# Two attention blocks, twice: the same operations issued in another order

## The chip, the core and the metric

The kernel runs on one core of one Trainium2 chip. The core has four engines that compute: TensorE (PE in the profile; PEld are its weight loads), VectorE (DVE), ScalarE (ACT) and GpSimd (POOL). SyncE (SP) issues most DMAs. Each engine works through its own instructions strictly in the order in which they were written, and waits at a semaphore where an instruction needs what another engine has yet to make. The metric is the device time of one execution in microseconds (us); lower is better. A time given for a kernel is the median of its runs.

## The reference

The input `x` has 2048 rows of 512 numbers, bf16. Four residual layers follow each other: A, B, A, B. Each normalises the rows, projects them to q, k and v for 32 heads of 16 columns, mixes, and projects back.

```python
x = x + A(layernorm(x))     # softmax attention over a window of 256 rows, causal
x = x + B(layernorm(x))     # linear attention: phi(q) @ sum(phi(k)^T v) / (phi(q) . sum(phi(k)))
x = x + A(layernorm(x))     # the same weights as the first A
x = x + B(layernorm(x))     # the same weights as the first B
# phi(t) = (t + 1 if t > 0 else exp(t)) + 1e-6
```

In layer A a row sees only 256 earlier rows, so the next B can begin on rows whose A is done. A row of B, though, needs the sum over all rows, so B's second half (dividing and projecting back) waits for the end of B's first half.

## The kernel before

The rows are cut into 16 tiles of 128, and four tiles make a block of 512; there are four blocks (I = 0 to 3) in each layer. Weights and the residual `xres` stay in SBUF. PSUM is one tensor `psb` of eight banks.

**A layer, block by block.** `ln_tile` (L661 and L662 statistics, L595 and L596 the inverse root on POOL) or `ln_sums` (L612 to L628) normalises a tile into `xn`; a DMA or PE transposes it into `xnT`. `proj` (L537) multiplies by a weight: four matmuls of 512 columns each into one bank, written as two half-steps of two matmuls that may stand apart. `evac` (L527) copies the bank out, on ACT or DVE; for the values it writes `vst`, for the queries `qT`. `k_spread` and `k_unit` (L773, L788) write the keys to `kall`; SP scatters the values from `vst` to `vbd` (L806).

**Scores and mixing.** A round of `scores` is one run of windows of 64 keys: PE multiplies keys and queries into four banks (L823), ACT takes the exponential of two banks (L834) and of the other two (L837), into one of seven buffers `pt`. Windows at the edge of the mask are set to zero: on POOL, one `affine_select` for each window (L857), or on DVE, one multiply by `tri` for one or two windows (L852). `pv_group` (L880) then multiplies `pt` by `vbd`, four steps of up to 12 small matmuls for a pair of tiles, and DVE divides (L893, L894) into `o_sb`, which is projected back and added to `xres` (L736 to L740). There are 156 rounds, 78 in each A layer. PE can begin a round when the exponentials of earlier rounds have emptied the four banks that it takes; ACT can begin the round's exponentials when PE is through with it.

**B layer.** Keys, values and queries are projected, `phi` is an exponential on ACT (L948), a clamp on DVE or POOL (L951) and a combination on DVE (L954). `kv_unit` (L995) sums keys times values; `kv_final` (L1042, L1051, L1063) makes the matrix `wkv` from it; `norm_pair` and `norm_unit` (L1078 to L1110) divide; `p2_tile` projects back, and in the last layer the rows go out (L720 to L731).

**What sets the order.** All of this is first noted down as 2583 operations with their needs, their possible engines and the buffers they take. Then `Planner.run` reads the string `ORDER` and issues them one by one. In it `692A` is operation 692 on ACT; the letters P, A, V, G and S stand for PE, ACT, DVE, POOL and SP; digits behind the letter are the buffers taken (for PE, mostly banks). `2F7` is no operation of the network: `fill` issues two matmuls of the identity into bank 7 (L463), whose result nobody reads. Nothing is reordered later, so the string alone fixes what stands behind what on each engine, which engine takes an operation that may go to several, and which bank or buffer it uses.

Four stages are spoken of below, cut at the start of a round on PE in the trace: the first A from its first round (10.9 us) to round 66 (135.1), the passage through B into the second A up to round 78 (135.1 to 205.7), the second A up to its last round (205.7 to 365.4), and the last B up to the end.

Of the kernel before, what the change touches and what calls it, by code (L numbers as in the profile page):

```python
# [214 lines left out]
24S 2G 5G 4G 15H 14H 53V0 0G 11G 58V1 17H 54A 68A1 6G 16H 63V2 3G 59G 55V20 18H 19H 1G 10F0 56P5 60V0 64G 61P1 57A 62V  # L215
9G 69V 2F2 74P0 75A 7V 1F2 70P1 65V0 72P6 71A 66P3 20H 92P7 73A 21H 67V 93P 120P42 94A 80P0 122A 95S 76P6 81V 88P1 121A
77V 89P 23H 22H 78P2 350V0 90A 123G 124P64 82P0 126A 79V 351G 91S 84P1 125A 340V1 133P24 83A 127G 96P6 85V 134A 106P0
10G 97V 104P1 135A 107V 137P26 341G 105V 139A 86P0 138A 146P46 87V 27S 116P1 147A 335V2 98P0 117P 148A 99V 336G 150P42
136V 25S 112P0 345V3 151A 149G 113P 152A 159P64 118A 337V31 140G 102P2 114V 161A 35S 128P1 346G 129P 103V 130P 131P 160A
342V1 163P42 153G 132V 26H 165A 115S 347V2 162G 3F0 188P06 164A 634V1 100P2 189A 166G 141P5 154P4 101V 155P 142P 36H  # L220
143P 190A 635G 144P 28H 352V0 193P02 145V 156P 119S 12G 157P 194A 108P6 158V 167P7 168P 191G 169P 195A 109V 170P 199P04
171V 348P6 200A 353P3 196G 349V 338P7 172S0 354V 343P6 201A 339V 204P02 638V0 379P7 29S 205A 380P 202G 344V 636V32 192G
206A 381V 2F5 210P04 361P6 639G 637S 642V1 362P 211A 208G 110P7 363V 212A 31S 203G 224P02 30H 198G 640V0 225A 383P5 213G
111V 384P 197V 382S 226A 643G 229P06 385V 214P4 215P 230A 646V0 216P 32H 358P5 644V3 231A 647G 217P 228V 235P02 641S
218V 359P 209G 236A 207G 355P7 360V 219P6 645S 237A 933V2 240P04 356P 241A 648V1 220P 239G 357V 221P 649S 232G 222P 233G
242A 246P02 227V 387P7 234G 386S 247A 223V 388P 238G 245V 389V 248A 395P04 13G 664P6 396A 665P 249V 934G 390S 250P7 667V
251P 397A 244G 400P02 666V 252P 243G 401A 941V0 253P 399G 391P6 392P 254V 402A 176S1 405P04 393V 364P7 406A 403G 365P
255P6 407A 366V 394S 410P02 256P 398V 257P 411A 404V 409G 258P 678P7 259V 412A 679P 416P04 680V 260S3 417A 657P3 414G
408V 415G 658P 276V 418A 650P2 264S2 660V 432P06 651P 413V 434A 419G 420V 51S 367P5 421V 368P 433A 659V 422P4 423P 369V
# [12 lines left out]
977P6 742A 554V 746P40 978P 748A 544P7 979V 545P 747A 744V 752P20 980S 745V 958P6 575V 754A 959P 750G 546V 735G 749V
269G 753A 2F5 768P40 960V 185G 751V 769A 755V 2F7 773P62 756V 757V 8V 774A 186G2 763P5 758P4 764P 567V0 775A 759P 187S
765P 559V1 760P 770A 766P 776G 761P 777G 275S 767V 778P26 270G1 955P0 779A 762V 956P 556P1 780A 957V 976S 783P42 557P
784A 782G 961P7 558V 962P 771G 785A 789P04 963V 985P6 271S 781G 790A 986P 786G 987V 791A 788G 183S 2F3 805P20 772G 787V
806A 793V 2F7 810P64 794G 37S 792V 812A 800P3 801P 802P 807A 795P5 803P 796P 811A 804V 797P 798P 571V2 38H 815P02 329P6
40H 813G 816A 46H 808G 799V 311P7 44H 50H 330P 560G 817A 52H 820P40 42H 331V 312P 821A 561G22 317P6 313V 822A 826P24
819V 809G 562S 318P 827A 548P7 824G 319V 549P 818G 823V 825G 828A 989P02 550V 814G 990A 831V 2F6 994P46 829G 830V 568G
995A 832P1 833P 834P 991A 835P 837P5 836V 838P 996A 839P 563V1 840P 842S0 1000P02 320A0 323P7 998G 841V 1001A 324P 564G
854S2 981P6 325V 1002A 1005P04 569G0 982P 999V 321V 1006A 964P7 983V 992G 965P 850S3 1007A 967P3 966V 1004G 968P 572G  # L250
332A3 1011P06 846S1 969V 843P5 1012A 1003G 844P 993G 855P4 1008V 984S 1013A 997G 1025P02 845V 856P 1010G 1009V 1027A
282P73 857V 283P 1026A 1014V 1030P24 858V3 277P62 570S 1031A 1015P0 322V 278P 988S 1016P 573V1 1032A 1017P 284V 1018P
279A 1036P24 1034G 1019V 1020P7 1038A 1021P 280V 1022P 281V 1023P 1037A 1041P04 1035V 290P60 1024V 1043A 291P 1040G
# [1195 lines left out]
```

## Time and profile before

| | before |
|---|---|
| time, median of 3 runs (lowest to highest) | 416.57 us (415.88 to 417.28) |
| profiled execution: span from first to last instruction | 414.3 us |
| median of the runs less that span | 2.3 us |
| busy PE / ACT / DVE / POOL | 395.2 / 368.8 / 355.0 / 239.2 us |
| mean granted clock of TensorE | 0.997 |

The profile is of one execution, whose own whole time is not listed; the 2.3 us beside its span is what lies around the first and last instruction if it was an ordinary one. Busy time of PE is the time in which some matmul is under way; as matmuls overlap, a PE that is busy may still be running with pauses. A stage's own figures say more than those of the whole: an engine that is busy for nearly all of a stage sets its length, whatever it does in others.

### The profile page before, as it was taken

How to read it: one execution, taken by the hardware profiler on the slowest of the kernel's cores; microseconds unless marked ns; L12 is line 12 of the kernel's file. 1: busy time of each engine (PE TensorE's matmuls, PEld its weight loads, DVE VectorE, ACT ScalarE, POOL GpSimd, SP SyncE). 2: the span in 40 equal slices, each digit the busy share in tenths (PEclk: the TensorE clock that was granted, in tenths of full speed). 3: DMA queues.
4: the chain of work that ended last, by engine and by line, in shares of the span. 5: the costliest groups of instructions: out<-in, count | busy, mean ns of one | idle time of the engine just before them, and what ended most of it. 6: DMA issues, size and time to landing. Idle time of an engine off the chain costs nothing.

```text
span 414.3 us, 15373 instructions
## 1 busy us (share of the span) xinstructions
PE 395.2 (95%) x6277; PEld 219.3 (53%) x6347; DVE 355.0 (86%) x844; ACT 368.8 (89%) x496; POOL 239.2 (58%) x505
## 2 busy tenths in 40 slices
PE   7998999999999999999999999999999999999995
PEld 3565555555555555643565555555555555565342
DVE  5899898888769988689998999998789588889895
ACT  5999999999999999678999999999999999977731
POOL 7578524344576667923774688554427476585432
PEclk9999999999999999999999999999999999999998
DMA  8233226440313122100032212322111311300024
GB/s 245 83 95 100 64 76 110 110 77 24 89 25 80 35 55 26 28 4 0 22 72 41 55 45 64 71 38 53 41 49 34 54 30 40 54 14 14 3 69 138
DMA packets 65306, 24.11 MB, mean 58 GB/s; under 512 B 46160, under 2 KB 65232, under 8 KB 65232
## 3 DMA queue, kind: packets, MB, share of 16 engines
q1 hardware_dynamic: 63168, 21.65, 23.5%
q10 hardware_dynamic: 2064, 1.44, 1.1%
q8 instruction: 50, 0.82, 0.8%
q14 instruction: 24, 0.20, 0.2%
HBM read 6.29 MB, written 2.10 MB: 20 GB/s over the span
## 4 chain that ended last, share of the span: by engine, by line
PE 66%; ACT 15%; DVE 12%; issue 4%; POOL 2%; ACTq 0%; POOLq 0%; DVEq 0%
PE psb L537 41%; PE psb L880 14%; PE psb L823 8%; ACT pt L834 7%; ACT pt L837 7%; DVE pt L852 2%; DVE kall L788 1%; PE psb L995 1%; DVE qT L527 1%; PE psb L566 1%; DVE kall L773 1%; PE psb L463 1%; DVE vst L527 1%; PE psb L1106 1%; DVE ln L661 1%
## 5 line engine op out<-in xcount | busy, mean ns | idle before, releaser
L857 POOL TENSOR_SCALAR_AFFINE_SELECT pt<-pt 128x256 bf16<-128x256 bf16 x285 | 121.3, 453 | 110.2 <-ACT pt L837 66.7
L837 ACT ACTIVATE pt<-psb 128x1024 bf16<-128x1024 f32 (+2 forms) x156 | 156.2, 1017 | 4.4 <-PE psb L823 3.0
L834 ACT ACTIVATE pt<-psb 128x1024 bf16<-128x1024 f32 (+2 forms) x156 | 156.7, 1014 | 3.6 <-PE psb L823 2.3
L880 PEld LDWEIGHTS <-pt 128*128 128x128 bf16 x2880 | 81.4, 96 | 16.5 <-issue 5.0
L880 PE MATMUL psb<-vbd,pt 128*128 128x34 bf16 x2880 | 85.1, 178 | 2.4 <-ACT pt L834 1.0
L537 PE MATMUL psb<-xnT,wA 128*128 128x512 bf16 (+1 forms) x305 | 65.1, 335 | 2.2 <-DVE o_sb L894 0.3
L537 PE MATMUL psb<-wB,xnT 128*128 128x512 bf16 x237 | 62.4, 379 | 1.7 <-issue 0.5
L823 PE MATMUL psb<-qT,kall 32*128 32x256 bf16 (+4 forms) x1664 | 62.6, 242 | 0.6 <-ACT pt L834 0.4
L537 PEld LDWEIGHTS <-xnT 128*128 128x128 bf16 x384 | 33.4, 97 | 37.0 <-issue 5.3
L823 PEld LDWEIGHTS <-kall 32*128 32x128 bf16 x1664 | 28.0, 92 | 45.8 <-issue 42.2
L852 DVE TENSOR_TENSOR pt<-pt,tri 128x512 bf16<-128x512 bf16 (+1 forms) x133 | 49.5, 399 | 2.8 <-ACT pt L837 1.9
L537 PEld LDWEIGHTS <-wA 128*128 128x128 bf16 x320 | 27.4, 97 | 26.1 <-issue 7.7
L537 PE MATMUL psb<-woA,oT 128*128 128x512 bf16 x120 | 32.8, 380 | 1.2 <-issue 0.6
L537 PE MATMUL psb<-wA,xnT 128*128 128x512 bf16 x115 | 32.3, 380 | 1.5 <-ACT pt L837 0.5
L537 PE MATMUL psb<-xnT,wB 128*128 128x512 bf16 x119 | 32.1, 380 | 0.9 <-issue 0.5
L537 PE MATMUL psb<-wkv,pqT 128*128 128x512 bf16 (+1 forms) x126 | 30.2, 373 | 0.5 <-issue 0.2
L894 DVE TENSOR_TENSOR o_sb<-psb,rall 128x256 bf16<-128x256 f32 x64 | 27.2, 424 | 2.4 <-DVE rall L893 0.2
L893 DVE RECIPROCAL rall<-psb 128x16 f32<-128x16 f32 x64 | 16.1, 251 | 13.7 <-PE psb L880 9.4
L661 DVE BATCH_NORM_STATS2 ln<-xres 128x6 f32<-128x512 f32 (+1 forms) x39 | 26.6, 682 | 1.2 <-DMA xres<-in_A_x_dram 1.1
L596 POOL TENSOR_TENSOR ln<-ln,mhalf 128x1 f32<-128x1 f32 x38 | 22.0, 578 | 3.2
L948 ACT ACTIVATE pks<-psb 128x512 bf16<-128x512 f32 x32 | 19.5, 614 | 3.8 <-PE psb L537 3.4
L527 DVE CAST qT<-psb 128x512 bf16<-128x512 f32 (+1 forms) x32 | 19.2, 602 | 3.9 <-PE psb L537 3.7
(133 smaller groups left out, 523.6 us busy)
## 6 DMA issues: line engine op xcount, KB each, us to landing
vbd<-vst SPq DMA_DIRECT2D x128, 34.0 KB, 1.9
wB<-in_B_wqkv_dram SPq DMA_DIRECT2D x6, 256.0 KB, 3.5
out_dram<-ost SPq DMA_DIRECT2D x10, 128.0 KB, 1.8
xres<-in_A_x_dram SPq DMA_DIRECT2D x4, 256.0 KB, 3.2
xnT<-xn SPq DMA_TRANSPOSE x50, 2.4
out_dram<-ost ACTq DMA_DIRECT2D x5, 128.0 KB, 2.8
wA<-in_A_wqkv_dram SPq DMA_DIRECT2D x1, 512.0 KB, 7.5
xres<-in_A_x_dram SPq DMA_DIRECT2D x1, 512.0 KB, 8.7
```

What stands on the lines that cost most here:

```text
L527: (nc.scalar.copy if e == "ACT" else nc.vector.tensor_copy)(dst(), src())
L537: nc.tensor.matmul(t["t"][:], lhsT=lhs(c), rhs=rhs(c), start=(c == 0), stop=(c == NCT - 1))
L596: nc.gpsimd.tensor_tensor(out, out, mhalf[:, 0:1], op=ALU.pow)
L661: nc.vector.bn_stats(t["st"], x())
L823: nc.tensor.matmul(psb[:, sT.k + x if x < 2 else sS.k + x - 2, at * 64:(at + w) * 64], lhsT=kbd[half(m)][32 * x:32 * x + 32, tt, m % 4, :, :],
L834: nc.scalar.activation(body[:, 0:2, 0:w_all, :], psb[:, sT.k:sT.k + 2, 0:w_all * 64].rearrange("p x (s c) -> p x s c", c=64), ACT.Exp, sca ...
L837: nc.scalar.activation(body[:, 2:4, 0:w_all, :], psb[:, sS.k:sS.k + 2, 0:w_all * 64].rearrange("p x (s c) -> p x s c", c=64), ACT.Exp, sca ...
L852: nc.vector.tensor_tensor(v, v, mt, op=ALU.mult)
L857: nc.gpsimd.affine_select(out=v, in_=v, compare_op=ALU.is_ge, fill=0.0, base=1 if kind == 0 else -2, pattern=[[0, 4], [2 * sg, 64]], chann ...
L880: nc.tensor.matmul(t["O"][:, x, g, :, :], lhsT=parts[b][0][:, s0:s0 + 2, :], rhs=vbd[half(m)][:, m % 4, :, 4 * tt + g, :], start=(n == 0), ...
L894: nc.vector.tensor_tensor(o_sb[:, u0:u0 + nu, P * tt:P * tt + P].rearrange("p u (h e) -> p u h e", e=DH), Ov[:, :, :, 0:DH], r.to_broadcas ...
L948: nc.scalar.activation(dst(), ps()[:], ACT.Exp)
```

## The change

Only the string `ORDER` is replaced. The earliest operations (the first 20 or so on each engine) keep their order, their engine and their buffers. All later ones are listed in another order, which a search over a planner's costs chose for the mean of six futures with delays drawn by chance. The operations, their code and their number are the same, with these differences:

- Of 19 `F` entries three stay, those at the very beginning: 13 filling matmuls of 45. The other 32 are gone.
- 217 of the 2583 operations go to another engine. 145 of these are masks: 74 go from POOL to DVE and 71 from DVE to POOL, which leaves POOL 204 in place of 207. By stage POOL's masks become 93 for 81 up to round 66, 15 for 20 in the passage, and 96 for 106 in the second A; DVE has the rest. ACT loses 26 operations and gains 20; none of the 312 exponentials of the scores changes engine.
- 558 operations take other banks of PSUM or other buffers.
- The 156 rounds of scores come in the same order, and in each of the four stages PE has the same work (but for the fills) to within two operations. What PE does between two rounds, and in which round ACT does its other work, changes all through the string.

The diff replaces the whole string; its lines tell little one by one. Two lines of each, out of the first A:

```diff
 ORDER = """
...
-656V 374P 938G 486A 681S 490P04 375V 690P6 483G 491A 691P 946G 487V 492A 177P7 489V 939V0 178P 488G 478V 506P02 692A
-494V 495G 493V 507A 693S 943V1 2F4 496P5 179V 501P4 508A 497P 511P06 498P 512A 510V 509G 502P 180V1 499P 47S 503P 513A
...
+656V 486A 482G 489G 487G 473V 490P06 375V 690P4 691P 488V 692V 491A 506P20 177P5 178P 492A 493V 494V 507A 495G 179V
...
 """
```

As the new string is three lines longer, every line of code below it has a number greater by three (L834 becomes L837, L837 becomes L840, L537 becomes L540, L852 becomes L855, L857 becomes L860). Each line below is one instruction of an engine, in its order: the line of code, the operation, what it writes and what it reads, and the shape.

The first place is on ACT in the first A, where the buffers `pt3` to `pt5` of three rounds are filled at about 68 us; `vst1` holds the values of one tile. Before:

```order
L834 ACTIVATE pt3_148<-psb_134 128x2x512
L837 ACTIVATE pt3_148<-psb_134 128x2x512
L834 ACTIVATE pt4_149<-psb_134 128x2x512
L837 ACTIVATE pt4_149<-psb_134 128x2x512
L527 CAST vst1_136<-psb_134 128x32x16
L834 ACTIVATE pt5_150<-psb_134 128x2x512
L837 ACTIVATE pt5_150<-psb_134 128x2x512
```

The same rounds on ACT afterwards:

```order
L837 ACTIVATE pt3_148<-psb_134 128x2x512
L840 ACTIVATE pt3_148<-psb_134 128x2x512
L837 ACTIVATE pt4_149<-psb_134 128x2x512
L840 ACTIVATE pt4_149<-psb_134 128x2x512
L837 ACTIVATE pt5_150<-psb_134 128x2x512
L840 ACTIVATE pt5_150<-psb_134 128x2x512
```

The copy of the values (operation 692) has left ACT; DVE has it now, between its masks of the first two of these rounds.

The second place is on PE in the first A, ahead of the scores of round 48 (operation 768, at 99.6 us before); `wA` is a weight, `identb` the identity that the fills multiply, `kall` the keys. Before:

```order
L537 LDWEIGHTS wA_67
L537 MATMUL psb_134<-xnT_1374,wA_67 128x512
L463 LDWEIGHTS identb_83
L463 MATMUL psb_134<-identb_83 128x512
L463 LDWEIGHTS identb_83
L463 MATMUL psb_134<-identb_83 128x512
L823 LDWEIGHTS kall_142
L823 MATMUL psb_134<-qT0_143,kall_142 128x192
```

The same place on PE afterwards:

```order
L540 LDWEIGHTS wA_67
L540 MATMUL psb_134<-xnT_1175,wA_67 128x512
L540 LDWEIGHTS wA_67
L540 MATMUL psb_134<-xnT_1175,wA_67 128x512
L826 LDWEIGHTS kall_142
L826 MATMUL psb_134<-qT0_143,kall_142 128x192
```

The two fills are gone, and the scores follow the projection at once.

The third place is on ACT in the second A, at round 101 (buffer `pt3`, at 262 us before). Before:

```order
L834 ACTIVATE pt3_148<-psb_134 128x2x512
L837 ACTIVATE pt3_148<-psb_134 128x2x512
L612 ACTIVATE xn_5495,lssq_168<-xres_71,lsum_167 128x512
L834 ACTIVATE pt4_149<-psb_134 128x2x512
L837 ACTIVATE pt4_149<-psb_134 128x2x512
```

The same rounds afterwards:

```order
L840 ACTIVATE pt3_148<-psb_134 128x2x512
L837 ACTIVATE pt3_148<-psb_134 128x2x512
L837 ACTIVATE pt4_149<-psb_134 128x2x512
L840 ACTIVATE pt4_149<-psb_134 128x2x512
L837 ACTIVATE pt5_150<-psb_134 128x2x512
```

The sum of squares of a tile (operation 2182) no longer stands between the exponentials of rounds 101 and 102; DVE does it. PE's work between the scores of these two rounds, six matmuls of L537 and 36 of L880, is the same before and after.

## Rows read from the trace of the kernel before

**Rows 1.** Page, part 1: busy us of each engine, share, instructions

```profile
PE 395.2 (95%) x6277; PEld 219.3 (53%) x6347; DVE 355.0 (86%) x844; ACT 368.8 (89%) x496; POOL 239.2 (58%) x505
```

**Rows 2.** Windows by stage: length, busy PE PEld DVE ACT POOL, clock, DMA

```profile
10.90:135.10 124.20, 119.25 (x2132) 70.28 (x2150) 105.85 (x252) 122.05 (x143) 67.63 (x160) 1.00 0.34 78
135.10:205.70 70.60, 69.47 (x976) 36.51 (x987) 61.71 (x153) 61.31 (x105) 43.32 (x75) 1.00 0.13 24
205.70:365.40 159.70, 155.16 (x2700) 88.68 (x2732) 139.81 (x327) 154.72 (x190) 97.76 (x218) 1.00 0.24 49
365.40:414.30 48.90, 43.02 (x438) 20.40 (x443) 41.18 (x86) 24.73 (x45) 22.73 (x26) 0.98 0.15 48
```

**Rows 3.** Waits of ACT, 10.9 to 135.1 us: total, times, longest

```profile
ACT pt L834 <- PE psb L823: 0.7, 3, 0.3
ACT pt L837 <- PE psb L823: 0.7, 1, 0.7
```

**Rows 4.** Waits of ACT, 205.7 to 365.4 us

```profile
ACT pt L834 <- PE psb L823: 1.6, 4, 0.8
ACT pt L837 <- PE psb L823: 1.2, 4, 0.4
```

**Rows 5.** Groups by shape: busy us, mean ns, idle before

```profile
L837 ACT ACTIVATE pt<-psb 128x1024 bf16<-128x1024 f32 x140 | 145.0, 1052 | 4.2 <-PE psb L823 3.0 <-POOL pt L857 0.6
L527 ACT CAST vst<-psb 128x512 bf16<-128x512 f32 x8 | 4.8, 600 | 0.2 <-PE psb L537 0.2
L527 ACT CAST qT<-psb 128x256 bf16<-128x256 f32 x6 | 2.3, 382 | 1.6 <-PE psb L537 1.6
L612 ACT ACTIVATE xn<-xres,lsum 128x512 bf16<-128x512 f32 x15 | 10.9, 727 | 3.1 <-DVE xres L736 1.9 <-issue 1.0
L857 POOL TENSOR_SCALAR_AFFINE_SELECT pt<-pt 128x256 bf16<-128x256 bf16 x285 | 121.3, 453 | 110.2 <-ACT pt L837 66.7 <-ACT pt L834 34.5 <-issue 3.3
L852 DVE TENSOR_TENSOR pt<-pt,tri 128x512 bf16<-128x512 bf16 x62 | 28.2, 463 | 1.4 <-ACT pt L837 0.8 <-ACT pt L834 0.5
```

**Rows 6.** Timeline, PE around round 48: start, length, instructions

```profile
98.22 1.04 PE L537 MATMUL psb<-xnT,wA 128*128 128x512 bf16 x4
99.09 0.59 PE L463 MATMUL psb<-identb 128*128 128x512 bf16 x2
100.00 0.61 PE L463 MATMUL psb<-identb 128*128 128x512 bf16 x2
```

**Rows 7.** Timeline, ACT over the same stretch

```profile
98.57 1.05 ACT L837 ACTIVATE pt<-psb 128x1024 bf16<-128x1024 f32 x1
99.47 2.90 ACT L834 ACTIVATE pt<-psb 128x1024 bf16<-128x1024 f32 x3
102.18 1.10 ACT L837 ACTIVATE pt<-psb 128x1024 bf16<-128x1024 f32 x1
```

**Rows 8.** Timeline, round 44, where ACT waits longest in the first A

```profile
94.42 0.40 PE L823 MATMUL psb<-qT,kall 32*128 32x320 bf16 x8
94.93 1.02 ACT L837 ACTIVATE pt<-psb 128x1024 bf16<-128x1024 f32 x1 [0.66 <-PE psb L823]
```

**Rows 9.** Chain of waits, pieces at rounds 44 and 101: start, us, what

```profile
91.97 2.53 PE psb L880 x96
...
259.26 1.40 PE psb L537 x6
...
262.39 0.91 PE psb L880 x36
```

**Rows 10.** Windows from the last division to the last matmul, and after

```profile
386.90:409.60 22.70, 21.89 (x118) 8.63 (x119) 21.53 (x34) 10.80 (x19) 9.43 (x8) 1.00 0.21 72
409.60:411.80 2.20, 0.00 (x0) 0.00 (x0) 0.66 (x1) 0.00 (x0) 0.00 (x0) 1.00 0.68 227
411.80:414.30 2.50, 0.00 (x0) 0.00 (x0) 0.00 (x0) 0.00 (x0) 0.00 (x0) 0.57 0.02 7
```

**Rows 11.** Page, part 4: the chain that ended last, by engine

```profile
PE 66%; ACT 15%; DVE 12%; issue 4%; POOL 2%; ACTq 0%; POOLq 0%; DVEq 0%
```

**Rows 12.** Timeline, the first fills

```profile
1.55 4.45 PE L463 MATMUL psb<-identb 128*128 128x512 bf16 x10 [1.55 <-POOL identb L392]
```

More of the change, by code (lines that the diff above doesn't have):

```diff
@@ L220 @@
[L220 to L229, printed above, removed]
@@ L340 @@
[L340 to L344 removed]
+24S 2G 5G 14H 53V0 4G 15H 0G 58V1 54A 16H 11G 17H 68A1 63V2 6G 3G 55V20 59G 10F0 56P5 57A 1G 60V0 18H 64G 61P1 19H 62V
@@ new lines @@
+1140P 1141P 1142P 1072S 1076S 879V 1148V 899P44 904P71 900P 1143V 894V 901A 1154P63 1149P22 1170P31 1171P 895V 1155V
+902V 903V 1150A 1156P6 1151P2 1152P 905P 1172A 906A 887V 1153V 1175P44 1157P 927P1 907P7 928P 1176P 1183P00 1158V
+1173V 1159A3 1160A 1164A1 1161V 929V 1174V 1184P 1162P1 1178P64 1179P 1165A 908V 1169V 1185V 619A0 1177A 1163A 1166G
+620V 621V 1180A 930A2 1167P5 1188P13 1193P31 1194P 1189P 931V 1181V 1182V 1168A 1190A 1196P00 1197P 1191V 1192V
+1201P52 1186P6 1202P 1206P4 909P2 1195A 1198A 1199V 1203A 1187V 1200V 1204P1 1205V 1226V 1228V 1240V 1207P 1216P3
@@ new lines @@
+1792V 2224V 1764S1 2209P6 2210P 1943A 1948P20 2211V 1760S2 1901P7 1902P 1949A 1941G 1931G 1945V 1947G 1946V 1936G
+1940V 1903V 1935G 1769P6 1950A 1964P42 1770P 1965A 1966A 1951V 1952V 1486P73 1487P 1953G 1771V 1959P1 1960P 1961P
+1784V1 1488A 1969P42 1954P0 1955P 1962P 1956P 1957P 1971A 1489V 1490V 1970A 1974P26 1963V 1958V 1975A 1765P4 1766P
+1976A 1979P02 1767V 1977V 1978V 2215P5 2216P 1980A 2218P4 2219P 1981A 2217V 1985P60 2220V 1761P5 1987A 1972G 1973G
+1785G 1968G 1479G0 1982G 1983G 1984G 1780V2 1762P 2225S 1484S 1480S 2221S 1494P40 1986A 1763V 1967V 2001P20 1495P
@@ new lines @@
+2002A 2003A 1990V 1989V 1499P52 1500P 1988G 1501V 1776V3 1991P7 1996P6 1997P 1496A 2006P02 2007A 1497V 1992P 1998P
+1999P 1993P 1994P 1498V 2008A 2011P04 1995V 2000V 2013A 1773P3 1774P 2012A 2016P64 1775V 1788V0 2226P2 2017A 2227P
+1507P30 2228V 2014G 2009G 2005V 2018A 1508P 2022P60 1515P24 1516P 2024A 2020V 2021V 1509V 1777G 1789G 2004G 2015G
+2010V 2023A 2038P04 1517V 2040A 1530P3 2039A 2025V 2027V 2026V 2019G 1778V10 1781G 2041V 1531P 1502P24 1503P 1790G0
+2043P64 1786G3 1782G2 1504A 2033P1 2028P0 2029P 2034P 2035P 2030P 2036P 2031P 1532A 1505V 2045A 1533V 1506V 1779S
@@ L345 @@
+2549P1 2550P 2577V1 2581V3 2568V0 2555A 2556G2 2557A 2574A 2547V3 2558P2 2559P 2551V2 2560V1 2578S 2582S 2569S 2548S
+2552S 2561S
 """
```

232 lines of the change are left out of this document (114 added, 118 removed).

## The prediction, made before the changed kernel was run

> **What bounds the kernel now.** I began with the busy times of the whole [rows 1]. PE is busy for 95% and ACT for 89%, but PE's figure counts a matmul until its modelled end, and PE can be slow while it only waits for a bank; so I went on to the windows by stage [rows 2]. In the first A ACT is busy for 122.05 of 124.20 us, in the second A for 154.72 of 159.70; there the exponentials set the pace. In the passage between them it is PE (69.47 of 70.60), ACT and DVE having 9 us of air. In the last B no engine is full over the whole stage, but from the last division to the last matmul DVE is (21.53 of 22.70 [rows 10]).
>
> The waits of ACT say how much PE costs it in the two A layers: 1.4 us in all in the first [rows 3], 2.8 in the second [rows 4]. So ACT has to be given less work, or these 4.2 us have to shrink, before the A stages get shorter; whatever else is taken from PE there only lets it wait for ACT sooner. One exponential takes 0.90 us of ACT in a row of them: five begin between 98.57 and 102.18 [rows 7], (102.18 - 98.57) / 4 = 0.90, though each lasts 1.05 alone [rows 5]. A round is thus 1.80 us of ACT. PE may be one round ahead, as a round takes four of eight banks, and by that lead a round with more work on PE can still be on time.
>
> **The fills.** Two matmuls of the identity last 0.59 or 0.61 us, four matmuls of the same 512 columns 1.04 [rows 6]; each further one costs (1.04 - 0.60) / 2 = 0.22 us. 32 times that is 7.0 us of PE. Where do they stand? 26 are in the first A, 4 in the second A and 2 in the last B. Around round 48 four of them run while ACT has no gap from 98.57 to 103.28 [rows 6, 7]. There they use time in which PE would wait for banks. I count them at 0; their cover is ACT's queue of exponentials. At most they could be worth the waits of ACT in the first A less the one at round 44, which has another cause (below), 1.4 - 0.66 = 0.7 us, plus 4 x 0.22 = 0.9 in the second A. [...]
>
> **First A.** ACT loses two casts of `vst`, 0.60 us each, and gets one of `qT`, 0.38 [rows 5]: -0.8 us, and as ACT is the bound that comes out in full. The price is on DVE and POOL. POOL gets 12 masks of one or two windows, 0.45 us a window [rows 5], 5 to 11 us more on 67.63 of 124.20; DVE sheds the same masks and takes the two casts, on 105.85 of 124.20 [rows 2]. Neither gets near the bound, but a mask of two windows is ready 0.9 us after the exponential on POOL and 0.46 on DVE, which `pv_group` may feel.
>
> At round 44 PE has eight steps of `pv_group` between two rounds, 96 small matmuls in 2.53 us [rows 9], 26 ns each, and ACT waits 0.66 us for the scores [rows 8]. In the new order three of these steps stand ahead of the scores before, and five are left: 60 x 26 ns = 1.6, with 0.3 for the scores 1.9 us, against 1.80 of ACT. Of the 0.66 I take 0.6 as won, with 0 and 0.66 as ends.
>
> **Passage.** PE is the bound and has the same work to within two operations (the fills are elsewhere): 0. DVE takes five masks from POOL, at up to 0.46 us each 2.3 us, and a little more; some 64 to 65 of 70.6. That is cover getting thin. Ends: -0.5 and +1.5, the latter if two or three of PE's steps find DVE late.
>
> **Second A.** ACT loses two of the squares, 0.73 us each [rows 5], and a cast, and gets two inverse roots, a cast and an exponential of `phi`; net -0.5 us. But a square that leaves helps only if PE is ready sooner. At round 101 PE has six projections (1.40 us) and 36 small matmuls (0.91) [rows 9] and about 0.25 for the scores between two rounds in either order: 2.5 us. ACT had 1.80 + 0.73 = 2.53 beside it and has 1.80 now: it will wait 0.7 us where it worked. I went through both orders in this way, round by round, with 0.22 us for a matmul of 512 columns, 26 ns for a small one and 0.90 for an exponential, and let PE's lead of one round pay what it can. What is left as lateness grows by 1.2 us in rounds 78 to 126 (101, 111 and 117 above all) and shrinks by 0.8 in rounds 126 to 155. With the -0.5 of work that makes -0.1; I take 0, ends -1.0 and +1.2.
>
> **Last B.** DVE's instructions from the last tile's division on add up to the same length in both orders, and it had no gap; PE's work up to there is the same. ACT takes two copies of the output rows, with half of the stage idle [rows 2]. 0, ends -0.3 and +0.8.
>
> **Sum.** -0.8 - 0.6 = -1.4 us on the profiled span of 414.3 gives 412.9. What lies around the span I take to be as before, the 2.3 us by which the median (416.57) exceeds it: 415.2. The ends together give about 413.0 to 418; as they won't all fall on one side, the forecast's own range is 413.5 to 416.6.
>
> **Rivals.**
>
> *Nothing measurable, 416.6.* A measurement of this kernel tells 0.3%, 1.25 us, from no change. The two terms of my sum are at that bound together, so any one of the upper ends above undoes it. For it: ACT's total work falls by only 0.7 us over the whole program. Against: the 0.66 us at round 44 has a plain cause that goes.
>
> *Bunched work on PE, slower, about 419.8.* Without the lead, the same count of rounds finds 22 of 155 before in which PE has over 0.12 us more work than ACT, by 7.0 us in sum, and 34 afterwards, by 11.65. Should PE not be ahead when such a round comes, the difference is paid in full: +4.65 - 1.4 = +3.2 us. The place is in the second A, rounds 101 to 137, and what takes the lead away would be a mask: on POOL two windows take 0.9 us where DVE took 0.46, and `pv_group` stands in front of the next scores. For it: before, 4.2 us of waits stand against the 7.0 of the count, 60% of it. Against: with the lead counted, the same count makes 4.4 before, close to those 4.2, and 5.1 afterwards. It eats the gain from 1.4 / 4.65 = 30% on and is a measurable loss from (1.4 + 1.25) / 4.65 = 57% on.
>
> *The fills were in the way after all, about 409.6.* The chain of waits is PE's for 66% [rows 11], and if all 32 fills lay on it the gain would be 7.0 us: 416.57 - 7.0 = 409.6. Against: ACT's gapless stretch around round 48. A part of it can well be true, 411 to 413.
>
> [...]
> [...]
>
> **How the numbers follow.** Forecast 0.34, of which 0.24 lies under 415.3 and 0.10 within 0.3%; no change 0.18; bunched work 0.28; fills in the way 0.17; clock 0.03. Faster: 0.24 + 0.17 = 0.41; same: 0.10 + 0.18 = 0.28; slower: 0.28 + 0.03 = 0.31. The range goes down to 411.0, past the likelier part of the fills' case, and up to 420.2, past the bunched case's 419.8; the clock and the full 7 us are left out.
>
> **What would show it.** In the changed profile ACT should be busy for about 121.2 us in the first A, which should be 122.5 to 123 us long; ACT's wait at round 44 should be under 0.1 us. PE should be less busy there, with pauses where the fills stood, at a clock of 1.00. The passage should stay at 70 to 71 us with DVE near 65. In the second A ACT should be about 154.2 us busy and wait longer for PE than 2.8 us, with new gaps of some 0.5 us at rounds 101, 111 and 117. From the last division to the end nothing should move. The forecast is wrong if the waits of ACT for the scores go beyond 6 us in sum, if the first A gets shorter by much more than 1.5 us (then the fills did cost), if PE waits for masks of POOL for more than 2 us, or if the clock leaves 1.00 before the end.

## The result and the profile after

The changed kernel takes 422.58 us (median of 6 runs, 421.71 to 425.93) against 416.88 for the kernel before (6 runs, 415.87 to 418.44). The ratio is 1.0148, 95% interval 1.0118 to 1.0178: slower by 6.2 us by the ratio. The forecast was 415.2, and the time lies above the range's 420.2. The profiled run took 422.81 us at a mean granted clock of 1.000, so the clock has no part in what its profile shows (in the run of 425.93 it was 0.985).

Busy times and the chain by engine, of the page after, answer to [rows 1, 11]:

```profile
PE 397.3 (94%) x6315; PEld 218.0 (52%) x6315; DVE 360.2 (86%) x852; ACT 366.8 (87%) x495; POOL 245.0 (58%) x501
...
PE 54%; DVE 15%; ACT 12%; POOL 8%; issue 5%; DMA 3%; SPq 1%; ACTq 0%; DVEq 0%; POOLq 0%
```

ACT's busy time fell by 2.0 us and the span grew by 6.7, so nothing was lost to more work on ACT. In the chain PE has 12 points less and ACT 3; POOL got 6, DVE and the DMAs 3 each: the work that comes last is theirs more often. The windows by stage (length; busy PE, PEld, DVE, ACT, POOL; clock, DMA), cut at the same rounds as [rows 2], but for the second cut, which lies 0.18 us behind the start of round 66 (137.37):

```profile
10.95:137.55 126.60, 117.19 (x2137) 69.61 (x2140) 104.74 (x243) 122.01 (x142) 78.83 (x183) 1.00 0.36 76
137.55:208.55 71.00, 70.86 (x988) 36.74 (x980) 64.16 (x156) 60.45 (x106) 41.88 (x63) 1.00 0.11 24
208.55:371.30 162.75, 158.08 (x2730) 87.72 (x2731) 143.75 (x341) 153.97 (x189) 98.19 (x214) 1.00 0.24 47
371.30:421.00 49.70, 43.36 (x441) 20.59 (x441) 41.15 (x86) 24.37 (x46) 18.38 (x16) 1.00 0.16 50
```

With that cut put right the stages grew by 2.2, 0.6, 3.05 and 0.8 us. In the first A ACT is nearly as busy as before (122.01 for 122.05, or 0.2 us less with the cut put right) in a stage that is longer, and in the second A it is busy 0.75 less: the difference of length and busy time, ACT's idle time, went from 2.15 to 4.59 and from 4.98 to 8.78. ACT's longest kinds of wait in the first A, then in the second (total, times, longest), against [rows 3, 4]:

```profile
ACT pt L840 <- PE psb L826: 1.9, 6, 0.5
ACT pt L837 <- PE psb L826: 0.9, 1, 0.9
ACT pt L840 <- issue: 0.6, 1, 0.6
...
ACT pt L837 <- PE psb L826: 3.9, 8, 0.9
ACT pt L840 <- PE psb L826: 2.2, 8, 0.5
```

So the scores come late, seven and sixteen times; one more gap in each stage is put down to `issue`. ACT's waits for the scores are 8.9 us in sum, for 4.2 before. What does PE wait for? The waits of PE over the whole program, after:

```profile
PE psb L883 <- DVE pt L855: 1.3, 4, 0.6
...
PE psb L826 <- DVE vst L530: 1.2, 1, 1.2
...
PE psb L540 <- DVE vst L530: 0.9, 2, 0.7
PE psb L826 <- DVE o_sb L897: 0.8, 2, 0.5
```

Before, the rows in which PE waits for DVE, from the first round on, were these:

```profile
PE psb L537 <- DVE o_sb L894: 0.3, 2, 0.2
PE psb L1063 <- DVE pks L569: 0.3, 1, 0.3
PE psb L537 <- DVE qT L527: 0.2, 1, 0.2
```

They add up to 0.8 us (0, 0, 0.5 and 0.3 by stage), and the rows of this kind after to 7.4 (4.0, 0, 2.4 and 1.0). Yet DVE has less to do in the first A than before (104.74 for 105.85). It is not fuller there; what PE needs comes later in its queue.

How many of ACT's gaps lie behind such a wait? The gaps of more than 0.15 us before its exponentials in the two A stages add up to 5.5 us before and 11.2 after. Those in front of which PE had waited for DVE since the scores of the round before make 0.2 us before and 5.3 after; those in front of which PE had not waited at all, 3.7 and 4.2. By the trace, most of the growth lies behind late steps of DVE, and little behind PE's work alone.

Last, the lag: the start of a round on PE, after less before. It is 0.05 us at round 0, 1.3 at 8, 1.6 at 16, 1.8 at 32, 2.4 at 64, 2.9 at 78, 3.6 at 104, 4.9 at 112, 4.4 at 132 and 5.8 at 155, and 0.85 more at the end. It comes in steps, one of them early and large, and falls back in places where PE has other work between the same rounds (0.5 at round 56, 2.5 at 58). The timeline after around that first step, round 7 (start, length, instruction, idle time before it):

```profile
19.78 1.94 DVE L675 TENSOR_SCALAR xn<-xres,ln 128x512 bf16<-128x512 bf16 x2
20.15 1.01 POOL L522 MEMSET vbd<- 128x1088 f32 x1
...
22.42 0.68 DVE L530 CAST vst<-psb 128x512 bf16<-128x512 f32 x1
...
23.15 0.27 PE L826 MATMUL psb<-qT,kall 32*128 32x64 bf16 x8 [1.20 <-DVE vst L530]
...
23.44 0.49 ACT L837 ACTIVATE pt<-psb 128x384 bf16<-128x384 f32 x1 [0.87 <-PE psb L826]
23.63 0.40 DVE L675 TENSOR_SCALAR xn<-xres,ln 128x512 bf16<-128x512 bf16 x1
```

Read it backwards. ACT waits 0.87 us for scores, which waited 1.20 for a bank that a copy of the values still had to empty. That copy stood on DVE behind normalisations. The first of the two at 19.78 takes 1.52 us, where one without company takes 0.40 (at 23.63), and from 20.15 to 21.16 POOL clears `vbd` beside it. In the kernel before the same work reads:

```profile
20.19 0.60 DVE L672 TENSOR_SCALAR xn<-xres,ln 128x512 bf16<-128x512 bf16 x1
20.72 0.68 DVE L527 CAST vst<-psb 128x512 bf16<-128x512 f32 x1
```

There the clearing (operation 13) stands some 140 entries further on in the string. In the new order the normalisation ends 0.14 us behind the clearing (21.30 and 21.16). That it takes longer beside the clearing is what the two timelines show; why, no row shows.

### The profile page after: what moved, and what is told of

Same layout as the page of the kernel before. It is cut to its first block, busy times and chain, and to the rows that moved or that the text cites. A ratio compares the mean times of both kernels' runs of the same rounds, so it can differ in the third digit from the quotient of the medians.

```text
span 421.0 us, 15381 instructions
## 1 busy us (share of the span) xinstructions
PE 397.3 (94%) x6315; PEld 218.0 (52%) x6315; DVE 360.2 (86%) x852; ACT 366.8 (87%) x495; POOL 245.0 (58%) x501
## 4 chain that ended last, share of the span: by engine, by line
PE 54%; DVE 15%; ACT 12%; POOL 8%; issue 5%; DMA 3%; SPq 1%; ACTq 0%; DVEq 0%; POOLq 0%
PE psb L540 34%; PE psb L883 11%; ACT pt L840 7%; PE psb L826 6%; ACT pt L837 4%; POOL pt L860 3%; DMA xnT<-xn 3%; DVE pt L855 2%; DVE pqT L1113 2%; POOL xn L631 2%; DVE kall L791 1%; PE psb L998 1%; DVE qT L530 1%; DVE ln L664 1%; POOL lrs L599 1%
## 5 line engine op out<-in xcount | busy, mean ns | idle before, releaser
L860 POOL TENSOR_SCALAR_AFFINE_SELECT pt<-pt 128x256 bf16<-128x256 bf16 x281 | 116.4, 445 | 91.3 <-ACT pt L837 46.6
L840 ACT ACTIVATE pt<-psb 128x1024 bf16<-128x1024 f32 (+2 forms) x156 | 155.1, 1008 | 7.4 <-PE psb L826 4.3
L837 ACT ACTIVATE pt<-psb 128x1024 bf16<-128x1024 f32 (+2 forms) x156 | 153.8, 1007 | 7.3 <-PE psb L826 6.3
L826 PE MATMUL psb<-qT,kall 32*128 32x256 bf16 (+4 forms) x1664 | 65.6, 242 | 5.1 <-DVE vst L530 1.2
L540 PE MATMUL psb<-xnT,wA 128*128 128x512 bf16 (+1 forms) x320 | 66.3, 337 | 3.1 <-ACT pt L840 0.9
L540 PE MATMUL psb<-wB,xnT 128*128 128x512 bf16 x256 | 63.9, 379 | 0.1
L826 PEld LDWEIGHTS <-kall 32*128 32x128 bf16 x1664 | 29.6, 92 | 52.1 <-issue 46.4
L855 DVE TENSOR_TENSOR pt<-pt,tri 128x512 bf16<-128x512 bf16 (+1 forms) x136 | 52.2, 409 | 3.9 <-ACT pt L837 1.6
L540 PEld LDWEIGHTS <-xnT 128*128 128x128 bf16 x384 | 33.4, 97 | 37.9 <-issue 5.2
L540 PEld LDWEIGHTS <-wA 128*128 128x128 bf16 x320 | 27.7, 97 | 27.5 <-issue 9.1
L540 PE MATMUL psb<-wA,xnT 128*128 128x512 bf16 x128 | 33.7, 380 | 0.8 <-ACT pt L840 0.5
L540 PE MATMUL psb<-woA,oT 128*128 128x512 bf16 x128 | 33.5, 380 | 0.5 <-DVE vst L530 0.2
L540 PE MATMUL psb<-xnT,wB 128*128 128x512 bf16 x128 | 33.5, 380 | 0.2 <-ACT pt L840 0.2
L540 PE MATMUL psb<-wkv,pqT 128*128 128x512 bf16 (+1 forms) x132 | 31.5, 373 | 0.3 <-DVE pqT L1113 0.2
L631 POOL TENSOR_SCALAR xn<-xres,lnm,lrs 128x512 bf16<-128x512 f32 x22 | 19.4, 882 | 9.3 <-ACT lrs L596 8.8
```

The costliest lines, as they stand in the source:

```text
L540: nc.tensor.matmul(t["t"][:], lhsT=lhs(c), rhs=rhs(c), start=(c == 0), stop=(c == NCT - 1))
L631: (nc.vector if e == "DVE" else nc.gpsimd).tensor_scalar(t["xn"][:], xres[:, i, :], lnm[:, c], lrs[:, c], op0=ALU.add, op1=ALU.mult)
L826: nc.tensor.matmul(psb[:, sT.k + x if x < 2 else sS.k + x - 2, at * 64:(at + w) * 64], lhsT=kbd[half(m)][32 * x:32 * x + 32, tt, m % 4, :, :],
L837: nc.scalar.activation(body[:, 0:2, 0:w_all, :], psb[:, sT.k:sT.k + 2, 0:w_all * 64].rearrange("p x (s c) -> p x s c", c=64), ACT.Exp, sca ...
L840: nc.scalar.activation(body[:, 2:4, 0:w_all, :], psb[:, sS.k:sS.k + 2, 0:w_all * 64].rearrange("p x (s c) -> p x s c", c=64), ACT.Exp, sca ...
L855: nc.vector.tensor_tensor(v, v, mt, op=ALU.mult)
```

## The experiments

A ratio is to the kernel before, timed on the same chip. Three theories stood against each other: that PE stood behind DVE's queue (late DVE), that PE's work between two rounds was bunched, and that the missing fills cost something.

**Before without its 32 later fills.**

```diff
-2F4 496P5 ... 3F7 521P06 ... 2F5 768P40 ... 2F7 773P62 ...
+496P5 ... 521P06 ... 768P40 ... 773P62 ...
```

> The kernel before with its 32 later fills left out and nothing else changed. Theory 'bunched PE' (the new order puts more of PE's work between two rounds, so ACT waits) and theory 'late DVE' (banks and masks that wait for DVE): the fills stood in PE's free time, 416 to 417.5 us, as before. Theory 'fills': without them PE is slower or its clock falls, 419 us or more, so a good part of the 5.7 us. The forecast's rival that the fills were in the way: 410 to 414.

1.0053 (1.0034 to 1.0072), 418.72 us. The fills are not dead weight: without them the kernel is 2.2 us slower. The profile, of an execution of 421.02 us, shows two things that are new. One is the clock, in windows of half a microsecond:

```profile
62.50:63.00 0.50, 0.50 (x27) 0.50 (x24) 0.22 (x2) 0.50 (x2) 0.00 (x0) 1.00 0.26 61
...
63.50:64.00 0.50, 0.50 (x24) 0.50 (x21) 0.00 (x0) 0.50 (x2) 0.00 (x0) 0.50 1.11 332
```

The granted clock falls to 0.50 from 63.3 to 66.7 us, although PE is busy in the whole of both windows. Just ahead PE had paused twice:

```profile
61.05 0.40 PE L826 MATMUL psb<-qT,kall 32*128 32x256 bf16 x8 [0.52 <-ACT pt L840]
...
61.97 2.75 PE L883 MATMUL psb<-vbd,pt 128*128 128x34 bf16 x96 [0.52 <-ACT pt L840]
```

In the kernel before, two pairs of fills stand at that place:

```profile
59.83 0.59 PE L463 MATMUL psb<-identb 128*128 128x512 bf16 x2
...
60.69 0.60 PE L463 MATMUL psb<-identb 128*128 128x512 bf16 x2
```

One pause of 0.52 us is left there before. Without the fills the clock is at 0.50 a second time, at 223.7 to 227.2 us, behind a pause of 1.66 us. That pause is the other new thing: PE waits for a DMA that transposes `xn`, and again for 1.55 us at round 131. The lag against the kernel before grows by 0.95 us over the first stretch, by 2.8 over the second with its pause, and by 1.1 at round 131. How much of the 2.2 us is the clock's is not told apart. The new order keeps a clock of 0.997 or more without fills in five of its six runs, so there the clock is not what it pays for.

The run also gives a fairer measure of late DVE. Without fills PE waits for DVE for 2.3 us in the old order too, where it was 0.8 with them, as some fills ran while it would have waited; of the 7.4 us after, some 5 are the new order's.

**The new order with the engines of before.** The 217 operations go back to their old engine, in the new places.

```diff
-107A ... 118V ... 136G ... 149V ... 191V ... 197G
+107V ... 118A ... 136V ... 149G ... 191G ... 197V
```

> The changed order with each of the 217 operations that changed engine put back on the engine of before; places in the list and banks as in the changed kernel. Theory 'late DVE': most of the loss goes, 416.5 to 419 us. Theory 'bunched PE': it stays, 421 to 424 us. Theory 'fills': stays, 422 us.

1.1113 (1.1054 to 1.1173), 461.74 us. The waits of PE:

```profile
PE psb L883 <- POOL pt L860: 9.9, 8, 3.3
PE psb L883 <- DVE pt L855: 4.0, 6, 1.1
```

An order and a choice of engines belong together, so this does not tell what the new choice is worth; it shows how long PE can stand before one mask on the wrong queue, 3.3 us.

**PE's order of one kernel with the rest of the other**, in both directions: PE's entries of one string are merged with all others of the other string. First PE's new order with the old rest (against the kernel before), then the reverse (against the new one).

```diff
-20H 92P7 73A 21H 67V 93P
+20H 73A 92P7 21H 93P 67V
...
-122A 95S 76P6 81V 88P1 121A
+122A 76P6 95S 88P1 81V 121A
```

> PE's order and its banks from the changed kernel, the order and the engines of everything else from the kernel before (113 of its operations moved by a few places where PE's order needs it); 32 fills out. Theory 'bunched PE': the loss comes with PE's order, 421 to 424 us. Theory 'late DVE': 416 to 419 us, as DVE and POOL have their old order.

> The other half: PE's order and banks from the kernel before (without the 32 fills), everything else in the order and on the engines of the changed kernel (89 operations moved by a few places). Theory 'bunched PE': 415.5 to 418 us. Theory 'late DVE': 420 to 424 us.

1.3346 (1.3266 to 1.3425), 556.86 us, and 1.3386 (1.3306 to 1.3466), 557.36 us in three of its four runs (566.02 in the fourth). Both expectations missed by far, and the two tell nothing apart: queues that were not laid out together stop each other (in the profile of the first DVE waits 43.0 us for PE's mixing, 9.4 before).

**The new order with DVE's needed work first**, at the six rounds where ACT waits longest behind a DVE step (7, 67, 85, 105, 107, 122). At round 7 the copy of the values (114) moves ahead of a copy of queries (103) and two normalisations (347, 352):

```diff
-150P06 337V01 347V2 152A ... 33S 29S 103V 352V1 151A 159P26 113P 30H ... 160A 114V
+150P06 337V01 152A ... 33S 29S 151A 159P26 113P 114V 103V 347V2 352V1 30H ... 160A
```

> The changed kernel with DVE's queue alone reordered at six rounds (7, 67, 85, 105, 107, 122), where the trace shows the scores of a round late behind a PE step that waits for DVE: the copy that empties the bank (or the mask) is put ahead of other work of DVE that nobody waits for. ACT's gaps at these rounds are 0.87, 0.60, 0.54, 0.55, 0.92 and 0.44 us, 3.9 in sum. Theory 'late DVE': half of that or more comes back, 418.5 to 420.8 us. Theory 'bunched PE': PE's work between the scores is the same, so 421.7 to 423.5 us.

1.0108 (1.009 to 1.0125), 421.25 us: by the ratios 1.7 us under the new order, with intervals that overlap, and between the two theories' ranges. The profile is of an execution of 423.21. PE's wait at round 7 fell from 1.20 to 0.19 us, but the work moved back was late in its turn (0.56 us for a transposed copy at 25.5). And at round 107 PE came to a mask of POOL:

```profile
267.07 0.94 PE L883 MATMUL psb<-vbd,pt 128*128 128x34 bf16 x31 [1.34 <-POOL pt L860]
```

Two microseconds on, the clock was at 0.50 there as well:

```profile
269.50:270.00 0.50, 0.50 (x20) 0.46 (x16) 0.12 (x1) 0.50 (x1) 0.28 (x1) 0.50 0.00 0
```

**Scores first**, at seven rounds where a `pv_group` step stands ahead of scores that come late:

```diff
-250P7 397A 251P 400P20 252P
+400P20 250P7 397A 251P 252P
```

> The changed kernel with PE's queue alone reordered at seven rounds (19, 34, 44, 102, 107, 112, 122): the scores stand ahead of the two or three pv steps that wait for a mask of DVE, which then follow them. Theory 'bunched PE': the same work has to be done one round later, so the gaps move on by a round, 421.5 to 423.5 us. Theory 'late DVE' (it is the wait in front of the scores that counts, not the work): the gaps of these rounds, 0.27, 0.48, 0.57, 0.79, 0.92, 0.50 and 0.44 us, shrink, 419 to 421 us.

1.0195 (1.0175 to 1.0215), 424.35 us: by the ratios worse by 2.0 us, and above both ranges. The wait moved one round on and grew: ACT waits 0.39 us at round 102 and 0.99 at 103, where it waited 0.79 at 102. That the gaps move on by a round is what the bunched-work theory had said of this edit.

**The two squares back on ACT** (2182 and 2190, the third place of the section on the change):

```diff
-2182V3 ... 2190V1
+2182A3 ... 2190A1
```

> The changed kernel with the two squares of rounds 101 to 105 (operations 2182 and 2190) back on ACT, nothing else changed. Theory 'late DVE': at round 105 the square waits 1.0 us in DVE's queue for a buffer that a DMA still reads, and holds up the copy that empties PE's bank; the 0.55 us gap goes, and ACT has the squares where it waited 0.79 and 0.55 us: -0.3 to -1.0 us, 421.6 to 422.3. Theory 'ACT is the bound' (the forecast's first step): two squares more on ACT, +0.5 to +1.4 us.

1.0142 (1.0123 to 1.016), 422.76 us: no change that can be told. The profile shows two effects against each other. The gap of 0.55 us at round 105 is gone; but PE now waits for ACT there (0.49 and 0.20 us) and for 0.79 us for a mask of POOL, and the lag grows by 1.7 us over rounds 104 to 108 in place of 1.1. So this run does not tell what 1.45 us of work on ACT are worth, nor that taking them off had won nothing.

**The new order with fills** at the places of before, in banks free there:

```diff
-770A 755G 773P06
+770A 755G 2F0 773P06
```

> The changed kernel with the 32 filling matmuls put back ahead of the same PE steps as before, each into a bank that is free there. Theory 'clock' (leaving them out costs 2 us by the clock, as it did in the kernel before): the mean granted clock goes up to 0.998 or more in all runs, and the time to 420.5 to 421.8 us. Theory 'order' (the clock of the changed kernel was 0.997 to 1.0 in most runs already): 422 to 423.5 us.

1.0193 (1.0179 to 1.0208), 424.71 us: by the ratios 1.9 us slower than without, of 7.0 us of matmuls, and above both ranges. In the profile the first A, where 26 of the 32 stand, is 2.3 us longer: PE is the late one there and pays for a part of them.

**PE's work spread**: at four rounds half a projection moves ahead of the scores before it.

```diff
-1904P3 1672A 1686P46 1905P 1687A
+1904P3 1672A 1905P 1686P46 1687A
```

> The changed kernel with PE's work spread at rounds 102, 107, 112 and 122: one half-projection (operations 1585, 1905, 1920, 1770; 0.43 us) moved ahead of the scores before, so that 2.50 us between two scores become 2.07 and the round before has 2.03 instead of 1.60, against 1.87 us of ACT (two exponentials). Nothing else changed. Theory 'bunched PE': ACT's gaps there (0.79, 0.92, 0.50, 0.44) shrink by up to 0.43 each, -1.0 to -1.7 us, 420.9 to 421.7. Theory 'late DVE': 422.3 to 423.2.

1.0147 (1.013 to 1.0164), 422.83 us: nothing, as late DVE said. Between rounds 100 and 126 the lag grows by 1.3 us, as much as with PE's order untouched (in the run below that moves the clearing). At these four places spreading PE's work won nothing.

**Both**, DVE's needed work first and PE's spread.

```diff
-159P26 113P 30H ... 160A 114V ... 1672A 1686P46 1905P
+159P26 113P 114V 103V 347V2 352V1 30H ... 160A ... 1672A 1905P 1686P46
```

> The edits of e5 (DVE's queue at six rounds) and of e9 (PE's work at four rounds) together. If both causes hold and add up: the 1.7 us that e5 brought and the 1.0 to 1.7 of e9, 419 to 420 us; if only late DVE holds: 421 us as e5.

1.0135 (1.0108 to 1.0163), 421.87 us, between the two; they don't add up.

**No masks on DVE**, in both kernels: `f_m` returns at once on DVE, so the windows that DVE should set to zero stay as they are.

```diff
 if e == "DVE":
+    return
     v = body[...]
```

> The kernel before without the masks that DVE makes (the 133 multiplies of L852, 49.5 us of DVE; those windows stay unmasked). A control for e12: it shows what the order of before is worth when DVE has time to spare. Both theories: PE hardly waits for DVE in it anyway (0.8 us in the profile), so 414 to 416.5 us.

> The changed kernel without the masks that DVE makes (136 multiplies of L855; those windows stay unmasked). Theory 'late DVE': with some 50 us of air on DVE the banks and inputs that PE waited for 7.4 us come in time, and the distance to e11 shrinks from 6 us to 2 us or less (2 being what the missing fills cost by the clock). Theory 'bunched PE' or any other cause in the order of PE and ACT: the distance stays at 4.5 us or more.

0.9974 (0.9961 to 0.9987), 415.86 us for the order before, and 1.0097 (1.007 to 1.0124), 420.53 us for the new one. Without DVE's masks the distance is 5.1 us in place of 6.2, by the ratios. That is the range of the other theories, 4.5 or more, and not the 2 or less of late DVE. But the waits did not go either: PE still waits for DVE for 5.4 us in the new order's profile. So DVE's 52 us of masks explain about one microsecond of the distance; its load is not the main cause, and whether the places in its queue are, this pair does not tell.

**More DVE work by need**: 18 DVE operations all over the new order move ahead of others that PE needs later.

```diff
-512A 505V 514V 500V ... 953P 712V 954V ... 769A 762V 778P06 ... 776G 767V
+512A 500V 505V 514V ... 953P 954V 712V ... 769A 778P06 ... 776G 767V 762V
```

> The changed kernel with 18 of DVE's operations put 1 to 4 places forward in DVE's queue, all over the program: those that PE waited for, ahead of work that nobody wants soon by the changed kernel's trace. Theory 'late DVE', if places in the queue are the cause: at least what six places brought in e5, 419 to 421.2 us. If it is DVE's whole load in a stretch and not the place: waits come back elsewhere, 421.5 to 423 us.

1.0123 (1.0103 to 1.0142), 422.9 us. It can't be told from no change, and the time is in the other theory's range: that each late copy can be mended by itself is not borne out.

**The clearing of `vbd` later in the new order**, at its place of before:

```diff
-101V 136G 13G 153G ... 389V 395P04
+101V 136G 153G ... 389V 13G 395P04
```

> The changed kernel with one operation of POOL moved: the third clearing of a values buffer (operation 13, a memset of 1.0 us), which runs at 20.15 us beside a copy of DVE that takes 1.52 us there and 0.40 elsewhere, goes back to its place of before (behind the masks at round 17). Theory 'DVE is held up by POOL in that stretch': the copy takes 0.4 to 0.6 us, DVE is 1 us earlier, ACT's 0.87 us gap at round 7 goes and the lag of rounds 7 to 20 (1.2 to 1.8 us) shrinks by 0.8 to 1.3: 421.3 to 421.9 us. Theory 'PE's and ACT's order': what is won there is given back by round 20, 422.3 to 423.

1.0132 (1.0104 to 1.016), 421.91 us. The timeline at round 7:

```profile
19.83 0.87 DVE L675 TENSOR_SCALAR xn<-xres,ln 128x512 bf16<-128x512 bf16 x2
...
22.19 0.27 PE L826 MATMUL psb<-qT,kall 32*128 32x64 bf16 x8 [0.19 <-DVE vst L530]
22.51 0.50 ACT L837 ACTIVATE pt<-psb 128x384 bf16<-128x384 f32 x1
```

Two normalisations take 0.87 us in place of 1.94, PE's wait goes from 1.20 to 0.19, and ACT's gap of 0.87 is gone. The lag at round 8 is 0.3 us in place of 1.3, and 1.0 is still there at round 104 (2.6 for 3.6). So the step is mended. In the whole time it shows as 0.7 us by the ratios, with intervals that overlap. Three of the six runs had a mean clock of 0.996 or more and took 420.1 to 421.3 us, the other three 0.993 to 0.994 and 422.5 to 423.4; the profile is of one of the first three, so where the clock fell in the others is not shown.

**The clearing early in the order before**, the counter-test:

```diff
-118A 337V31 140G ... 395P04 13G 664P6
+118A 337V31 13G 140G ... 395P04 664P6
```

> The kernel before with one operation of POOL moved: the third clearing of a values buffer (operation 13, 1.0 us) stands where the changed order has it, ahead of the masks of round 5 and so at about 20.2 us, beside a copy of DVE (L672 at 20.19, 0.60 us). Nothing else changed, the fills included. Theory 'DVE is held up by POOL there': the copy takes 1.0 to 1.5 us, the copy of the values behind it is late and ACT waits at round 7: +0.5 to +1.3 us, 416.9 to 417.8. If the old order has time to spare there: 416.2 to 416.7.

1.0019 (1.0005 to 1.0033), 417.1 us: 0.8 us slower (0.2 to 1.4 by the interval), by one POOL instruction moved. The profile is of an execution of 419.22, in which already round 0 comes 1.2 us late; over rounds 7 to 9 the lag grows by 0.5 more.

```profile
21.43 1.19 DVE L675 TENSOR_SCALAR xn<-xres,ln 128x512 bf16<-128x512 bf16 x1
21.47 1.01 POOL L522 MEMSET vbd<- 128x1088 f32 x1
...
23.60 0.26 PE L826 MATMUL psb<-qT,kall 32*128 32x64 bf16 x6 [0.53 <-DVE qT L530]
23.94 0.49 ACT L840 ACTIVATE pt<-psb 128x384 bf16<-128x384 f32 x1 [0.39 <-DVE xn L675]
```

The normalisation beside the clearing is slow in this order as well: 1.19 us for 0.60 before, and it ends 0.14 us behind the clearing again (22.62 and 22.48). Scores and exponential wait.

**Three combinations**: the clearing later with all six DVE places; with four of them (without rounds 7 and 107); and these with eight fills besides. Of each kind of edit one place (the last only in the third kernel):

```diff
-136G 13G 153G ... 389V 395P04 ... 1029G 1028V 292V ... 755G 773P06
+136G 153G ... 389V 13G 395P04 ... 1029G 292V 1028V ... 755G 2F0 773P06
```

> e14 and e5 together. If the two add up (1.7 us of e5, 0.8 to 1.3 of e14, less what both take at round 7): 419.8 to 420.8 us. If not, 421.2 as e5.

> e14 (the clearing moved) with DVE's queue reordered at rounds 67, 85, 105 and 122 as in e5, but without e5's edits at round 7 (e14 covers it) and at round 107 (there the masks put ahead made PE wait 1.34 us for a mask of POOL, and the clock fell behind that pause in e5 and e15). Theory 'late DVE': e14 and what is left of e5 add up, 419.8 to 420.9 us in executions in which the clock holds. Theory 'PE's and ACT's order': no better than e14, 421.5 to 422.5.

> e16 with 8 of the 32 fills put back, two each ahead of the scores of rounds 49, 53, 54 and 59, where PE has nothing but scores between two rounds and pauses about 0.5 us. Theory 'the clock falls behind such pauses': clock 0.997 or more in every execution, median 0.5 to 1.5 us below e16. Theory 'fills cost their time' (all 32 cost 1.9 us in e8): 0.4 to 0.9 us above e16.

1.0159 (1.0135 to 1.0183), 422.66 us; 1.0129 (1.0095 to 1.0163), 421.89; 1.0122 (1.0092 to 1.0152), 421.97. None adds to the clearing alone. In the first all six runs had a mean clock of 0.989 to 0.994, in the others five and four of six were under 0.996. In all three profiles the clock falls at about 268 us: with six places it is at 0.50 for 3.4 us, behind a pause of 1.33 us for a mask of POOL; with four, and with the fills besides, its mean is 0.77 and 0.81 from 265 to 270 us and 0.88 and 0.85 from 270 to 275. In the profile of the four places PE pauses twice there, 0.43 us for a mask of DVE and, two matmuls later, 0.79 for one of POOL. The eight fills stand in the first A, far ahead of this fall. In the one run of the four places in which the clock held (0.997) the time was 421.67, so the late-DVE sum of 419.8 to 420.9 did not come out there either. No version of the new order beats the kernel before.

## Why the prediction was wrong

The step that failed is the first A's "Neither gets near the bound", and the same cover in the other stages. It judged DVE by its busy share, 105.85 of 124.20. The share was right, even lower afterwards, and said nothing about when a copy is done that PE's next scores wait for. The time that PE waits for DVE went from 0.8 to 7.4 us (2.3 without fills in the old order), and ACT's idle time in the two A stages grew by 2.4 and 3.8. Of these 6.2 us ACT's smaller work takes 1.0 back, and the other two stages add 0.6 and 0.8: the span's 6.7, up to rounding. The prediction had named the sign: it is wrong if ACT's waits for the scores go beyond 6 us in sum, and they are 8.9.

- **The lead.** "PE may be one round ahead" was behind every item costed at nothing. At round 7 it paid 0.33 us: a wait of 1.20 on PE became a gap of 0.87 on ACT.
- **First A, -0.8.** ACT's busy time fell by 0.2 us in that stage, not 0.8, and the stage grew by 2.2 us, of which the clearing beside a normalisation is 0.9 to 1.0, by the lag at rounds 8 and 104 with and without it.
- **Round 44, -0.6.** The steps went ahead as read, but the gap moved with them, one round earlier:

```profile
93.55 0.97 PE L883 MATMUL psb<-vbd,pt 128*128 128x34 bf16 x32 [0.28 <-DVE pt L855]
...
94.45 0.40 PE L826 MATMUL psb<-qT,kall 32*128 32x256 bf16 x8
...
94.95 1.02 ACT L840 ACTIVATE pt<-psb 128x1024 bf16<-128x1024 f32 x1 [0.57 <-issue]
```

  0.57 us for the 0.66 of [rows 8]. The scores now stand behind the moved steps, and these behind a mask of DVE, for 0.28 us. The releaser is given as `issue`, but the scores end at 94.85 and ACT begins 0.1 later.
- **Passage, 0.** Inside its ends: 0.6 us longer from round 66 on, with DVE at 64.16 in the window above.
- **Second A, 0.** ACT's work fell by 0.75, near the 0.5. The new gaps came where the count had them (its 101, 111 and 117 are 102, 112 and 118 in the trace's numbers), 0.5 to 0.8 us long:

```profile
256.87 1.02 ACT L837 ACTIVATE pt<-psb 128x1024 bf16<-128x1024 f32 x1 [0.79 <-PE psb L826]
...
278.42 1.02 ACT L837 ACTIVATE pt<-psb 128x1024 bf16<-128x1024 f32 x1 [0.51 <-PE psb L826]
...
290.61 1.02 ACT L840 ACTIVATE pt<-psb 128x1024 bf16<-128x1024 f32 x1 [0.65 <-issue]
```

  Other gaps the count did not have, for it counted lengths and no waits. Round 105 is one: the square 2190, now on DVE, waits for a buffer that a DMA reads, and a copy that PE needs waits behind it; in the clearing run's profile, among others, the lag at this round is some 0.85 us better.

```profile
260.31 0.75 DVE L617 SCALAR_TENSOR_TENSOR xn<-xres,lnm 128x512 bf16<-128x512 f32 x1 [1.01 <-DMA xnT<-xn]
260.99 0.69 DVE L530 CAST vst<-psb 128x512 bf16<-128x512 f32 x1
...
261.73 1.02 PE L540 MATMUL psb<-xnT,wA 128*128 128x512 bf16 x4 [0.69 <-DVE vst L530]
```

- **Last B, 0.** It grew by 0.8, the upper end given.
- **Fills, 0.** Wrong for the order before, where taking them out costs 2.2 us, by the clock, by waits for a DMA, or by both; not the cause in the new order as profiled. For the clock, to which the prediction gives a chance of 0.03, no run shows a time of its own: the runs showed a clock of 0.50 for two stretches of 3.4 us in the old order without fills, and a mean of 1.000 in the new order's profile.
- **The bunched-work rival** gave the direction and, at 419.8, about half of the size. Its places in the second A show up, but spreading work at four rounds gave nothing, the gaps without any wait of PE grew by 0.5 us only, and what it named as taking the lead away, a mask of POOL, is not seen: PE waits for POOL in one row of the profile after, for 0.4 us. The late steps are copies and masks of DVE.
- **The range.** The ends of the stages add up to about 413.3 to 419.3, not to "413.0 to 418"; the time lies above either. And ACT loses 21 operations in the change, not 26.

Shown by a run that changes one thing: the clearing (1.0 us of the lag, 0.8 in the order before) and the cost of DVE's masks (1.1 by the ratios). Read from the traces and not shown by an edit: that the rest, some 4 us, is made mostly of late DVE steps, spread over rounds 8 to 155 and the tail. The two sizes need not add up. The edits do not settle it: apart from the clearing, of those that set late DVE against PE's order only the spread of PE's work gave late DVE's time. Moving DVE's steps forward gave back 1.7 us at most, with intervals that overlap, as the edits that mended a wait let the next one come out or made PE stop at a mask of POOL. The 558 changed banks and buffers were not tried by themselves. So the cause of the rest stays open.

## What to carry to other kernels

An engine's busy share tells whether it can do its work, not whether the work is done in time (DVE's in the first A fell from 105.85 to 104.74 us, and PE's waits for it rose from 0 to 4.0): list what the pacing engine's next step needs, and count what stands before it in each queue. Where order, engines and banks were laid out together, expect a change of one alone to cost much (11 to 34% here) and a mend at one place to bring out the wait behind it. Before a filling matmul is taken out, see what the clock and the waits do in its place (32 of them out cost the order before 2.2 us), and before one is put in, whether PE is the late engine (32 in cost the new order 1.9). Where a profile is of an execution well off the median, compare its rounds from the start before a step in it is put down to the edit.

## What the runs showed of the hardware

- Stretches at a granted clock of 0.50 came after short pauses of PE, but not after each of them. In the order before without fills two pauses of 0.52 us, 0.40 us of work apart, were followed by 3.4 us at 0.50, of which PE was busy for some 3.2, and one of 1.66 us by another 3.4 us. In the new order with DVE's needed work first one of 1.34 us was followed by 3.4 us as well. Yet the new order has a pause of 1.20 us at round 7 and its profile has a mean clock of 1.000, while nearly the same pause at the same round (1.17 us) was followed by a fall in the profile of the new order without DVE's masks (mean clock 0.99 from 20 to 25 us, 0.67 from 25 to 30). In the profile of the spread, which has the new order there, the mean clock was 0.57 from 25 to 30 us. In the order before without fills the lag grew by 0.95 us across the first stretch, and by 2.8 across the second with the pause of 1.66 in it.
- A normalisation on DVE (`TENSOR_SCALAR`, 128x512 bf16, 0.40 us) took 1.19 (order before with the clearing early) and 1.52 us (new order) beside a clearing of 1.01 us on POOL, and ended 0.14 us behind the clearing both times.
